# Filter stage of a spectral mixer: inverse step five groups behind, five buffers, earlier weight split, a new order of the last groups

## The chip, the cores and the metric

The kernel runs on one core of a Trainium2 chip. The metric is device time in microseconds of one execution. The core has five engines that run beside each other, each with its own queue worked off in order: TensorE (PE in the profile; PEld is its weight load), VectorE (DVE), ScalarE (ACT), GpSimd (POOL), and SyncE (SP), which here only issues DMAs. TensorE writes its products to PSUM, which the kernel uses as four tiles; ACT and DVE read them, POOL does not in this kernel.

## The reference

Four layers on x of 2048 x 640 float32: filter, MLP, filter, MLP, each with a layer norm ahead and a residual. Only the filter's part is touched.

```python
def _A_ref(x, w_r, w_i):
    W = w_r + 1j * w_i
    X = jnp.fft.rfft2(x, axes=(-2, -1)) * W
    return jnp.fft.irfft2(X, s=(S, D), axes=(-2, -1))
x = x + _A_ref(_layernorm(x), A_w_r, A_w_i)
x = x + _B_ref(_layernorm(x), B_w1, B_b1, B_w2, B_b2)   # twice, both
```

## The kernel before

Transforms are products with tables of cosines and sines, and each operand is split into a float16 high part and a float16 low part (h and l), so that three products give about float32. Sums in PSUM are float32.

The filter of one layer is made in three steps. `a0` (before, and inside the MLP stage ahead of the second filter) makes the first factor of the transform over the 2048 rows. `a1`, the stage that is changed, runs over NG = 16 groups of rows; for each group g it makes the transform over the 640 columns, the second factor over the rows, the product with the filter, and the inverse of the second row factor. `a2` then makes the inverse over the columns and the last inverse factor, adds the residual and normalises for the MLP. `a1` and `a2` run once for each of the two filter layers; the last stage before the second `a1` is the end of the first MLP.

In `a1` one group goes through these steps, named by functions inside it:

- `dstage(g)`: TensorE, columns, from `s1h`, `s1l` and the small stack `stk`; result in PSUM.
- `psplit`: ACT makes `ph`, DVE makes `pl` from that PSUM tile.
- `s2stage(g)`: TensorE, forward step over rows (table `tS2`).
- `terms`: DVE, two passes over PSUM with the filter `w` and a scale `sx`, into `ta`, `tb`; `sums`: POOL, two passes, real and imaginary part of the product.
- `xhi`: ACT, `xh`; `xlo`: POOL, `xl`; `twice`: ACT, a copy of 63 columns inside `xh` (0) or `xl` (1), which the inverse needs twice.
- `is2stage(g)`: TensorE, inverse step over rows (table `tI2`, 36 products with half of the rows each), into PSUM.
- `yhi`: ACT, `Yh`; `ylo`: DVE, two passes, `Yl`. All groups' Y together are the operand of `a2`, whose first product (`id_mm(0)`) therefore waits for the last group.

The loop is software-pipelined and its order is fixed: while `self.pin` is set, each engine's instructions keep the order of the program. DMAs of SP are not pinned; a planner places them. In the pass g of the loop (g = 0 to 14) TensorE does `dstage(g+1)`, `is2stage(g-3)`, `s2stage(g)`; ACT `xhi(g-2)`, its copy, `ph` of g+1, `yhi(g-3)`, the copy of `xl`; POOL `xlo(g-2)`, `sums(g-1)`; DVE `terms(g-1)`, `pl` of g+1, `ylo(g-3)`. The tiles `xh`, `xl` have three buffers (`xs`, index g % 3). After the loop, groups 12 to 15 are still to be inverted; that end is written out by hand.

Beside this, the loop prepares the first weight tile of the MLP that follows: `wload(0)` loads it as two halves `raw`; in the first layer `scan1` squares each half on ACT and `scale_b` and `scale1` make a power of two as its scale, each with one tiny product with `ones` into a PSUM tile of its own and then a chain of tiny DVE operations; `wsplit` splits the tile in four quarters, `wh` on ACT and one pass later `wl` on DVE. The MLP's loads of tile 1 go into the same two `raw` buffers. PSUM tiles all come from one pool of four (`big`); a tile that is asked for waits until one has been read.

Of the kernel before, what the change touches and what calls it, by code (L numbers as in the profile page):

```python
# [12 lines left out]
AF = mybir.ActivationFunctionType  # L13
# [4 lines left out]
S, D, NL, F = 2048, 640, 321, 1728  # L18
NJ, NG, NFT = 16, 16, 14
NQ = 8  # L20
SEQ = [t + 7 * i for t in (0, 6, 1, 2, 3, 4, 5) for i in range(2)]
EPS = 1e-5
GC = 0.044715
# [34 lines left out]
class Layers:  # L58
# [41 lines left out]
    def setup(self):  # L100
# [16 lines left out]
        self.qt = base.tile([128, NFT], F32, name="qt")  # L117
        self.s2, self.c2 = (base.tile([128, NQ], F32, name=f"{a}p") for a in "sc")
        self.second, self.nr = False, 3
# [300 lines left out]
    def a1(self, first):  # L420
        nc, A = self.nc, self.A
        V, G, T = self.V, self.G, self.T
# [6 lines left out]
        self.tDi = pY.tile([128, 2, 3, 2, 322], F16, name=f"tDi{self.n}")  # L429
        p = self.push("a1", side=self.sp)  # L430
        xs = []
        for i in range(3):
            xh = p.tile([128, 2, 384], F16, name=f"xh{i}_{self.n}")
            xl = p.tile([128, 2, 384], F16, name=f"xl{i}_{self.n}")
            xs.append((xh, xl))
# [6 lines left out]
        def yparts(g, ps, lt):  # L442

            o = tuple(y[:, g, :, lt.start * 32:lt.stop * 32] for y in yv)
            return pairs(ps, lt.start * 128, lt.stop * 128), *o

        def yhi(g, ps, lt=slice(0, 3)):
            a, h, _ = yparts(g, ps, lt)
            T.activation(h, a, AF.Copy, scale=YC)

        def ylo(g, ps, lt=slice(0, 3)):
            a, h, l = yparts(g, ps, lt)
            for q in range(2):
                V.scalar_tensor_tensor(l[:, q], a[:, q], YC, h[:, q], op0=ALU.mult, op1=ALU.subtract)
# [46 lines left out]

        def xhi(g, c, x):

            return T.activation(xs[g % 3][0][:, :, c], x, AF.Copy)

        def xlo(g, c, x, W=G):

            xh, xl = (q[:, :, c] for q in xs[g % 3])
            return W.tensor_tensor(xl, x, xh, op=ALU.subtract)

        def twice(g, i):

            q = xs[g % 3][i]
            T.activation(q[:, :, NL:], q[:, :, 257:320], AF.Copy)

        def s2stage(g, ph, pl):
# [9 lines left out]
        def is2mm(ps, g, lt):  # L526

            sp = 1 if g == 0 else 0
            out = slice(128 * lt, 128 * lt + 128)

            for ri in range(2):
                for k, (a, b) in enumerate(((0, 0), (0, 1), (1, 0))):
                    for q in range(2):
                        r = slice(64 * q, 64 * q + 64)
                        mm(
                            ps[:, q, out], xs[g % 3][a][r, ri, out], self.tI2[r, b, sp, ri],
                            start=ri == 0 and k == 0, stop=ri == 1 and k == 2,
                        )

        def is2stage(g):  # L540
            ps = self.big()
            for lt in range(3):
                is2mm(ps, g, lt)
            return ps

        def s2mm(ps, x, lt):

            c = slice(128 * lt, min(128 * lt + 128, NL))
            for ri in range(2):
                for q in range(2):  # L550
                    a = tuple(self.tS2[:, h, 0, 2 * ri + q] for h in range(2))
                    self.mm3(ps[:, ri, c], a, tuple(b[:, q, c] for b in x), q == 0, q == 1)
# [8 lines left out]
        def sums(tt, c, W=G):  # L561

            ta, tb = (q[:, :, c] for q in tt)
            W.tensor_tensor(ta[:, 0], ta[:, 0], tb[:, 1], op=ALU.subtract)
            return W.tensor_tensor(ta[:, 1], tb[:, 0], ta[:, 1], op=ALU.add)
# [8 lines left out]
        quarter = lambda q: ((q // 2,), slice(q % 2 * 4, q % 2 * 4 + 4))  # L574

        self.pin = True
        every = slice(0, NL)
        w = {g: wload(g) for g in range(3)}
        pp, ps2, pv, ta = {}, {}, {}, {}
        ps = dstage(0)  # L580
        pp[0] = tuple(self.t(p, [128, 2, 322], F16, a, 2) for a in ("ph", "pl"))
        sc = PQS / (S1S * TS)
        for q in range(2):
            a, b, c = ps[:, q, :NL], pp[0][0][:, q, :NL], pp[0][1][:, q, :NL]
            T.activation(b, a, AF.Copy, scale=sc)
            V.scalar_tensor_tensor(c, a, sc, b, op0=ALU.mult, op1=ALU.subtract)
        for g in range(NG - 1):
            q = psplit(dstage(g + 1))
            if g > 2:
                pv[g - 3] = is2stage(g - 3)  # L590
            ps2[g] = s2stage(g, *pp.pop(g))
            i = g % NC
            if i:
                stack(g + 3)
            k = g - 1
            if first and g == 0:
                for _ in self.scale_x(p):
                    pass
            if k > 0:
                xhi(k - 1, every, ta[k - 1])  # L600
                twice(k - 1, 0)
                xlo(k - 1, every, ta.pop(k - 1))
            if k >= 0:
                tt = terms(ps2.pop(k), k, w[k])
                ta[k], gi = tt[0], sums(tt, every)
            next(q)
            pp[g + 1] = next(q)
            if 10 <= g < 14:
                self.wsplit(0, quarter(g - 10)[0], hi=False, part=quarter(g - 10)[1])
            if k == 3:  # L610
                with self.after(gi):
                    nc.gpsimd.dma_start(self.tDi, A["tDi"])
                    nc.gpsimd.dma_start(self.tIM0, A["tIM"][:, 0:4])
            if g > 2:
                yhi(g - 3, pv[g - 3])
                ylo(g - 3, pv.pop(g - 3))
            if k > 0:
                twice(k - 1, 1)
            if k >= 0 and g + 2 < NG:
                w[g + 2] = wload(g + 2)  # L620
            if g == 3:
                self.wload(0)
                self.wopen(0)
            if first and g == 4:
                sb = self.scale_b()
            if first and 4 <= g < 8:
                next(sb)
            if first and g in (5, 6):
                self.scan1(0, (g - 5,))
            if first and g == 7:  # L630
                sc0 = self.scale1(0)
            if first and 7 <= g < 10:
                next(sc0)
            if 9 <= g < 13:
                self.wsplit(0, quarter(g - 9)[0], lo=False, part=quarter(g - 9)[1])

        k = NG - 2
        parts = slice(0, 256), slice(256, NL)
        h = self.big()
        for lt in range(3):  # L640
            s2mm(h, pp[k + 1], lt)
        xhi(k - 1, every, ta[k - 1])
        twice(k - 1, 0)
        xlo(k - 1, every, ta.pop(k - 1))
        tt = terms(ps2.pop(k), k, w[k])
        ta[k] = tt[0]
        sums(tt, every)
        twice(k - 1, 1)
        pv[k - 2] = is2stage(k - 2)
        tt = [self.t(p, [128, 2, NL], F32, a, n) for a, n in (("ta", 3), ("tb", 2))]  # L650
        for c in parts:
            for i, q in enumerate(tt):
                filtered(q[:, :, c], h[:, :, c], k + 1, w[k + 1][:, :, c], i)
            sums(tt, c, V if c.start else G)
        xhi(k, every, ta[k])
        twice(k, 0)
        yhi(k - 2, pv[k - 2])
        pv[k - 1] = is2stage(k - 1)
        for c in parts:
            xhi(k + 1, c, tt[0][:, :, c])  # L660
            xlo(k + 1, c, tt[0][:, :, c], V)
        twice(k + 1, 0)
        xlo(k, every, ta.pop(k))
        ylo(k - 2, pv.pop(k - 2))
        twice(k, 1)
        twice(k + 1, 1)
        pv[k] = is2stage(k)
        yhi(k - 1, pv[k - 1])
        ylo(k - 1, pv.pop(k - 1))
        h = [self.big() for _ in parts]  # L670
        is2mm(h[0], k + 1, 0)
        is2mm(h[0], k + 1, 1)
        yhi(k, pv[k])
        ylo(k, pv.pop(k))
        is2mm(h[1], k + 1, 2)
        for q, lt in zip(h, (slice(0, 2), slice(2, 3))):
            yhi(k + 1, q, lt)
            ylo(k + 1, q, lt)
# [130 lines left out]
    def wtile(self, m):  # L809

        k, i = m // NFT, m % NFT if m < NFT else m - NFT
        if self.second:
            i = i // 2 + i % 2 * NQ if k else SEQ[i]
        return min(k, 1), i, NFT if k else NJ
# [282 lines left out]
    def b2nd(self, li):  # L1097
# [17 lines left out]
        for j in range(NJ):  # L1115
            self.h.append((self.hh[j], ph.tile([128, 2, 320], F16, name=f"hl{j}_{self.n}")))
            V.tensor_tensor(self.h[j][1], self.hf[j], self.hh[j], op=SUB)
        V.tensor_tensor(self.s2, self.st[1][:, :NQ], self.st[1][:, NQ:], op=ALU.min)
        V.tensor_tensor(self.c2, self.ct[1][:, :NQ], self.ct[1][:, NQ:], op=ALU.max)
        self.pin = False  # L1120
# [19 lines left out]
        UB = {a: i for i, a in enumerate(("B11", "B21", "B22", "T1", "T2", "T3", "T4"))}  # L1140
        ops = [(d, *q) for d in range(NQ) for q in PQ]
        NP = len(ops)
# [67 lines left out]

        dup = lambda m: SEQ[m] == NFT - 1

# [19 lines left out]
        for m in range(NFT):  # L1232
            t, k = SEQ[m] % 7, SEQ[m] // 7
            if m < 2:
# [8 lines left out]
            for j in run:  # L1243
# [8 lines left out]
                if m == NFT - 1 and j in (1, 4, 7, 10):  # L1252
# [434 lines left out]
```

## Time and profile before

| what | us |
|---|---|
| three runs | 1034.32, 1034.83, 1036.58; median 1034.83 |
| profiled execution, its own time | 1035.71 |
| its span, first to last instruction | 1033.9 |
| first `a1`: first column product to the next stage's first product | 60.6 to 135.5 |
| second `a1` | 567.7 to 638.8 |
| busy in the span: PE, DVE, ACT, POOL | 987.5, 724.0, 571.2, 263.8 |
| granted TensorE clock, mean over the span | 0.977 |

How to read the rows that follow. A timeline row is start, duration, engine, line, operation, output<-inputs, shapes, count; in brackets the idle time of that engine just before and what ended it. Nearly all rows have line 50, the line of a helper through which pinned instructions are recorded, so they are told apart by the names of their tiles: `ta`, `tb` are the filter's terms, `ps` a PSUM tile. A row of the chain of waits is start, duration, what. A row of stretches has the stretch, its length, busy time and count for PE, PEld, DVE, ACT, POOL, then the granted clock, the DMA share and GB/s. Ends of matmuls are modelled, and neighbouring instructions overlap a little, so durations here are taken from start to start.

### The profile page before, as it was taken

Reading aid. Unit: us, or ns where it says so; the run is one execution under the profiler, and the core shown is the slowest. Engines: PE = TensorE matmul, PEld = TensorE weight load, DVE = VectorE, ACT = ScalarE, POOL = GpSimd, SP = SyncE. Lnnn points to the kernel's source line nnn. Section 1 sums busy time; section 2 is a strip of 40 time slices with the busy share of each in tenths; the row PEclk is TensorE's granted clock in tenths of the full one; section 3 lists DMA queues with packets and bytes.
Section 4 is the critical chain, followed back from the end, with each engine's and each line's share of the span. In section 5 each row is a group of like instructions: output and inputs, shape, how many; then the busy total and the mean of one; then the engine's idle time right before and its main releaser. Section 6 shows DMA issues by size and latency. Waiting matters only on the chain.

```text
span 1033.9 us, 20948 instructions
## 1 busy us (share of the span) xinstructions
PE 987.5 (96%) x8379; PEld 737.1 (71%) x8379; DVE 724.0 (70%) x1424; ACT 571.2 (55%) x874; POOL 263.8 (26%) x436
## 2 busy tenths in 40 slices
PE   4879989999999999999997998999999999999998
PEld 3767767677777777777775887776777777777776
DVE  7978968954333956666675797897654564988885
ACT  4847668675554556555542475784544454534541
POOL 6928747500000002222112575770000000000000
PEclk9599999999999999999998999999999999999999
DMA  7765356622222264444412644655322232445411
GB/s 227 276 180 165 109 160 220 209 85 93 78 79 75 71 237 146 138 135 123 123 59 73 195 148 132 199 186 196 127 85 82 73 107 78 140 153 174 163 44 52
DMA packets 55738, 139.48 MB, mean 135 GB/s; under 512 B 6461, under 2 KB 12249, under 8 KB 55641
## 3 DMA queue, kind: packets, MB, share of 16 engines
q1 hardware_dynamic: 54200, 131.97, 39.7%
q0 software_dynamic: 1440, 6.17, 1.9%
q8 instruction: 66, 1.08, 0.4%
q14 instruction: 32, 0.25, 0.1%
HBM read 115.05 MB, written 23.07 MB: 134 GB/s over the span
## 4 chain that ended last, share of the span: by engine, by line
PE 55%; DVE 18%; ACT 9%; POOL 8%; issue 5%; DMA 4%; SPq 0%; ACTq 0%; POOLq 0%; DVEq 0%
PE ps L50 55%; DMA xt<-x 4%; DVE wl L50 3%; DVE st L50 3%; DVE f L50 2%; DVE s1l L50 2%; POOL eo L50 2%; POOL ta L50 2%; DVE xt L50 2%; ACT wh L50 2%; POOL xt L50 1%; ACT z L50 1%; ACT junk L50 1%; DVE hl L50 1%; ACT eh L50 1%
## 5 line engine op out<-in xcount | busy, mean ns | idle before, releaser
L50 PEld LDWEIGHTS <-wh 128*128 128x128 f16 x2992 | 289.7, 98 | 113.1 <-issue 1.8
L50 PEld LDWEIGHTS <-wl 128*128 128x128 f16 x1616 | 157.9, 98 | 62.4 <-DVE wl L50 0.9
L50 PE MATMUL ps<-hh,wh 128*128 128x320 f16 x896 | 186.5, 299 | 0.7 <-ACT hh L50 0.6
L50 PE MATMUL ps<-hl,wh 128*128 128x320 f16 x896 | 184.7, 299 | 0.0
L50 PE MATMUL ps<-hh,wl 128*128 128x320 f16 x832 | 171.5, 299 | 0.5 <-DVE wl L50 0.5
L50 DVE SCALAR_TENSOR_TENSOR wl<-raw,s,wh 128x1024 f16<-128x1024 f32 (+2 forms) x88 | 105.3, 1201 | 87.6 <-ACT wh L50 87.5
L50 PE MATMUL ps<-uh,wl 128*128 128x320 f16 x448 | 133.1, 299 | 0.0
L50 PE MATMUL ps<-ul,wh 128*128 128x320 f16 x448 | 133.1, 299 | 0.0
L50 ACT ACTIVATE wh<-raw,s 128x1024 f16<-128x1024 f32 (+2 forms) x92 | 94.7, 1047 | 68.4 <-PE ps L50 61.6
L50 PE MATMUL ps<-uh,wh 128*128 128x320 f16 x416 | 124.3, 299 | 0.0
L50 ACT ACTIVATE junk<-raw 128x896 bf16<-128x896 f32 (+1 forms) x60 | 59.6, 994 | 45.5 <-DMA raw<-w 45.4
L50 PE MATMUL ps<-tDi,Yh 128*128 128x322 f16 x320 | 71.6, 301 | 0.4 <-ACT Yh L50 0.4
L50 POOL TENSOR_TENSOR r<-v,mh 128x1 f32<-128x1 f32 x64 | 37.3, 584 | 133.6 <-DVE nm L50 123.3
L50 PE MATMUL ps<-u,wo 128*128 128x320 f16 x504 | 69.9, 299 | 0.0
L50 DVE TENSOR_TENSOR f<-eo 128x256 f32<-128x256 f32 (+1 forms) x124 | 39.0, 368 | 41.9 <-POOL eo L50 41.2
L50 PEld LDWEIGHTS <-wo 128*128 128x128 f16 x504 | 49.3, 98 | 19.1
L50 POOL TENSOR_TENSOR xt<-xt,ec 128x320 f32<-128x320 f32 x64 | 52.4, 840 | 38.6 <-DVE xt L50 38.5
L50 DVE BATCH_NORM_STATS2 st<-xt 128x6 f32<-128x320 f32 x126 | 55.3, 481 | 6.3 <-DMA xt<-x 5.2
L50 ACT ACTIVATE z<-xt,nb,r 128x640 f32<-128x640 f32 x31 | 28.5, 919 | 56.0 <-POOL z L50 43.5
L50 PE MATMUL ps<-tM,f 128*128 128x128 f32 x160 | 38.3, 415 | 21.5 <-DMA xt<-x 12.2
L50 PE MATMUL ps<-ph,tS 128*128 128x321 f16 (+2 forms) x288 | 58.0, 286 | 0.1
L50 POOL TENSOR_TENSOR eo<-z 128x320 f32<-128x320 f32 x62 | 53.2, 880 | 17.1 <-ACT z L50 15.1
(175 smaller groups left out, 1880.6 us busy)
## 6 DMA issues: line engine op xcount, KB each, us to landing
raw<-w SPq DMA_DIRECT2D x56, 512.0 KB
xt<-x SPq DMA_DIRECT2D x79, 320.0 KB
w<-w SPq DMA_DIRECT2D x48, 321.0 KB
x<-xt SPq DMA_DIRECT2D x47, 320.0 KB
raw<-w SPq DMA_DIRECT2D x32, 448.0 KB
raw<-w2z SPq DMA_DIRECT2D x32, 448.0 KB
out<-xt SPq DMA_DIRECT2D x15, 320.0 KB
tIM<-tIM POOLq DMA_DIRECT2D x8, 512.0 KB, 5.6
```

What stands on the lines that cost most here:

```text
L50: i = f(*a, **k)
```

## The change

The inverse step, `Yh` and `Yl` follow five groups behind instead of three (`LAG`), `xs` has five buffers (`NX`). The load of weight tile 0, its squares, its scale and its split move two passes ahead; `scale_b`, and the DMAs that POOL issues in the loop, stay. After the loop six groups, 10 to 15, are to be inverted, and the order of that end is new: two inverse steps stand before the sums of group 14, each `Yh`, `Yl` pair (`back`) stands between the steps of groups 14 and 15, the upper columns of group 15 go ahead of the lower ones.

```diff
+LAG, NX = 5, 5
-        for i in range(3):
+        for i in range(NX):
             xh = p.tile([128, 2, 384], F16, name=f"xh{i}_{self.n}")
...
-            return T.activation(xs[g % 3][0][:, :, c], x, AF.Copy)
+            return T.activation(xs[g % NX][0][:, :, c], x, AF.Copy)
...
-            if g > 2:
-                pv[g - 3] = is2stage(g - 3)
+            if g >= LAG:
+                pv[g - LAG] = is2stage(g - LAG)
...
-            if 10 <= g < 14:
-                self.wsplit(0, quarter(g - 10)[0], hi=False, part=quarter(g - 10)[1])
+            if 8 <= g < 12:
+                self.wsplit(0, quarter(g - 8)[0], hi=False, part=quarter(g - 8)[1])
...
-            if g > 2:
-                yhi(g - 3, pv[g - 3])
-                ylo(g - 3, pv.pop(g - 3))
+            if g >= LAG:
+                yhi(g - LAG, pv[g - LAG])
+                ylo(g - LAG, pv.pop(g - LAG))
...
-            if g == 3:
+            if g == 1:
                 self.wload(0)
                 self.wopen(0)
...
-            if first and g in (5, 6):
-                self.scan1(0, (g - 5,))
-            if first and g == 7:
+            if first and g in (3, 4):
+                self.scan1(0, (g - 3,))
+            if first and g == 5:
                 sc0 = self.scale1(0)
-            if first and 7 <= g < 10:
+            if first and 5 <= g < 8:
                 next(sc0)
-            if 9 <= g < 13:
-                self.wsplit(0, quarter(g - 9)[0], lo=False, part=quarter(g - 9)[1])
+            if 7 <= g < 11:
+                self.wsplit(0, quarter(g - 7)[0], lo=False, part=quarter(g - 7)[1])
...
+        def back(n):
+            yhi(n, pv[n])
+            ylo(n, pv.pop(n))
+
+        n = k - LAG + 1
...
+        pv[n] = is2stage(n)
+        pv[n + 1] = is2stage(n + 1)
         sums(tt, every)
         twice(k - 1, 1)
-        pv[k - 2] = is2stage(k - 2)
         tt = [self.t(p, [128, 2, NL], F32, a, n) for a, n in (("ta", 3), ("tb", 2))]
         for c in parts:
             for i, q in enumerate(tt):
                 filtered(q[:, :, c], h[:, :, c], k + 1, w[k + 1][:, :, c], i)
-            sums(tt, c, V if c.start else G)
+        sums(tt, parts[1], V)
+        back(n)
+        pv[n + 2] = is2stage(n + 2)
+        sums(tt, parts[0])
         xhi(k, every, ta[k])
         twice(k, 0)
-        yhi(k - 2, pv[k - 2])
-        pv[k - 1] = is2stage(k - 1)
-        for c in parts:
-            xhi(k + 1, c, tt[0][:, :, c])
+        xhi(k + 1, parts[1], tt[0][:, :, parts[1]])
+        twice(k + 1, 0)
+        back(n + 1)
+        pv[n + 3] = is2stage(n + 3)
+        xlo(k, every, ta.pop(k))
+        xhi(k + 1, parts[0], tt[0][:, :, parts[0]])
+        back(n + 2)
+        for c in parts[::-1]:
             xlo(k + 1, c, tt[0][:, :, c], V)
-        twice(k + 1, 0)
-        xlo(k, every, ta.pop(k))
-        ylo(k - 2, pv.pop(k - 2))
         twice(k, 1)
         twice(k + 1, 1)
+        back(n + 3)
         pv[k] = is2stage(k)
-        yhi(k - 1, pv[k - 1])
-        ylo(k - 1, pv.pop(k - 1))
         h = [self.big() for _ in parts]
         is2mm(h[0], k + 1, 0)
         is2mm(h[0], k + 1, 1)
-        yhi(k, pv[k])
-        ylo(k, pv.pop(k))
         is2mm(h[1], k + 1, 2)
+        back(k)
         for q, lt in zip(h, (slice(0, 2), slice(2, 3))):
             yhi(k + 1, q, lt)
             ylo(k + 1, q, lt)
```

More of the change, by code (lines that the diff above doesn't have):

```diff
@@ L502, in xhi @@
         def xhi(g, c, x):
-            return T.activation(xs[g % 3][0][:, :, c], x, AF.Copy)
+            return T.activation(xs[g % NX][0][:, :, c], x, AF.Copy)
         def xlo(g, c, x, W=G):
-            xh, xl = (q[:, :, c] for q in xs[g % 3])
+            xh, xl = (q[:, :, c] for q in xs[g % NX])
             return W.tensor_tensor(xl, x, xh, op=ALU.subtract)
         def twice(g, i):
-            q = xs[g % 3][i]
+            q = xs[g % NX][i]
             T.activation(q[:, :, NL:], q[:, :, 257:320], AF.Copy)
@@ L535, in is2mm @@
                         mm(
-                            ps[:, q, out], xs[g % 3][a][r, ri, out], self.tI2[r, b, sp, ri],
+                            ps[:, q, out], xs[g % NX][a][r, ri, out], self.tI2[r, b, sp, ri],
                             start=ri == 0 and k == 0, stop=ri == 1 and k == 2,
```

## The prediction

> **What bounds the kernel now.** I read the page first, then the chain of waits through both filter stages, then the engines' timelines there. On the page TensorE is busy 96% of the span, and both filter stages end in a hole of it. A pass is one turn of the loop over g; X is the moment at which a pass starts its `xl` on POOL.
>
> ```profile
> PE 987.5 (96%) x8379; PEld 737.1 (71%) x8379; DVE 724.0 (70%) x1424; ACT 571.2 (55%) x874; POOL 263.8 (26%) x436
> ```
>
> The chain of waits, second filter stage (start, us, what): in the loop it runs from POOL's sums to ACT's `xh`, to POOL's `xl` and to sums again, and not through TensorE; it comes back to TensorE at 640.04, with the next stage's first products.
>
> ```profile
> 627.84 1.47 POOL ta L50 x2
> 629.33 0.75 ACT xh L50
> ...
> 640.04 5.03 PE ps L50 x35
> ```
>
> Undisturbed this ring takes 3.69 us a pass, as POOL's timeline shows, each `xl` waiting for ACT:
>
> ```profile
> 89.64 1.42 POOL L50 TENSOR_TENSOR xl<-ta,xh 128x642 f16<-128x642 f32 x1 [0.85 <-ACT xh L50]
> ...
> 93.33 1.42 POOL L50 TENSOR_TENSOR xl<-ta,xh 128x642 f16<-128x642 f32 x1 [0.85 <-ACT xh L50]
> ...
> 601.74 1.42 POOL L50 TENSOR_TENSOR xl<-ta,xh 128x642 f16<-128x642 f32 x1 [0.85 <-ACT xh L50]
> ```
>
> TensorE's own pass is longer: forward step over s from 599.01, column step (D) from 600.66, inverse step (I) from 601.90, forward step again from 603.01. That is 4.00 us, 1.11 of it inverse step.
>
> ```profile
> 599.01 0.31 PE L50 MATMUL ps<-ph,tS 128*128 128x321 f16 x1
> ...
> 600.66 0.30 PE L50 MATMUL ps<-tD,s1h 128*128 128x160 f16 x2
> ...
> 601.90 0.29 PE L50 MATMUL ps<-tI,xh 64*128 64x128 f16 x4
> ...
> 603.01 0.31 PE L50 MATMUL ps<-ph,tS 128*128 128x321 f16 x1
> ```
>
> So TensorE falls 0.31 us a pass behind the ring and at last holds it: ACT waits 0.41 for an inverse step, with a weight split and the next `xh` queued behind it. Later VectorE paces the passes with a weight quarter, 4.15 us from `pl` to `pl` (619.17 to 623.32), with no idle time in between.
>
> ```profile
> 607.13 0.81 ACT L50 ACTIVATE Yh<-ps 128x768 f16<-128x768 f32 x1 [0.41 <-PE ps L50]
> ```
> ```profile
> 619.17 0.82 DVE L50 SCALAR_TENSOR_TENSOR pl<-ps,ph 128x642 f16<-128x642 f32 x1
> 619.90 0.97 DVE L50 SCALAR_TENSOR_TENSOR wl<-raw,s,wh 128x512 f16<-128x512 f32 x1
> 620.80 1.01 DVE L50 SCALAR_TENSOR_TENSOR Yl<-ps,Yh 128x384 f16<-128x384 f32 x2
> 621.73 0.87 DVE L50 SCALAR_TENSOR_TENSOR ta<-ps,sx,w 128x642 f32<-128x642 f32 x1
> ...
> 623.32 0.81 DVE L50 SCALAR_TENSOR_TENSOR pl<-ps,ph 128x642 f16<-128x642 f32 x1
> ...
> 629.11 0.87 DVE L50 SCALAR_TENSOR_TENSOR ta<-ps,sx,w 128x642 f32<-128x642 f32 x1
> ...
> 632.99 0.67 DVE L50 TENSOR_TENSOR ta<-tb,ta 128x65 f32<-128x65 f32 x1
> 635.35 0.94 DVE L50 TENSOR_TENSOR xl<-ta,xh 128x512 f16<-128x512 f32 x2 [1.69 <-ACT xh L50]
> 636.22 4.16 DVE L50 SCALAR_TENSOR_TENSOR Yl<-ps,Yh 128x384 f16<-128x384 f32 x10
> ```
>
> **The loop, second stage.** Passes 3 and 4 lose their inverse step, so TensorE gains 2 x 1.11 = 2.2 us of lead. It loses 0.31 a pass from pass 5 on, so the lead lasts seven passes, to pass 12, and the slower weight passes stretch that. Hence ACT no longer waits at 607.13. Up to pass 8 (X = 601.74) nothing changes, since the ring sets those passes. The four weight passes are now 8 to 11: 4 x 4.15 brings X to 618.3, two ring turns of 3.69 to 625.7 in pass 14. `pl` follows X by 0.89 (94.22, in the fence of the first stage below, after 93.33), and `ta` of group 14 follows `pl` by 0.73 + 0.93 (619.17 to 619.90, 620.80 to 621.73): 628.2 against 629.11, 0.9 gained. Bounds: nothing (if the quarters alone made the old passes late) and 1.4 (if the first of the four costs the ring its 3.69 alone).
>
> **The last groups, second stage.** Count from that `ta` (t = 0; PE resumed at 640.04, so 10.93 before). VectorE now has five groups of `Yl` at 0.93 (620.80 to 621.73) instead of three. Until 4.55 its order is the old one (632.99 + 0.67). `Yl` 10 fills the old hole, 4.55 to 5.48. From here ACT sets the time:
>
> ```profile
> 633.02 0.74 ACT L50 ACTIVATE xh<-ta 128x642 f16<-128x642 f32 x1 [1.10 <-POOL ta L50]
> 633.80 0.31 ACT L50 ACTIVATE xh<-xh 128x126 f16<-128x126 f16 x1
> 634.01 0.79 ACT L50 ACTIVATE Yh<-ps 128x768 f16<-128x768 f32 x1
> 634.70 0.83 ACT L50 ACTIVATE xh<-ta 128x512 f16<-128x512 f32 x2
> ```
>
> By starts: a whole `xh` 0.78, a copy 0.21, a `Yh` 0.69 (its output after 0.79), the two parts of `xh` 15 0.83, with the wait of a copy for its input 0.86, which I part into 0.34 and 0.52. ACT starts `xh` 14 at 3.91 as before; then copy, small part, copy bring it to 5.45; `Yh` 11 is out at 6.24, so VectorE idles 0.76; large part, `Yh` 12 out at 7.45, VectorE idles 0.28 after `Yl` 11; `Yl` 12 ends at 8.38; `xl` 15 takes 0.87 (635.35 to 636.22), to 9.25. The copy of `xl` 15 stands ahead of `Yh` 13 in ACT's queue and waits for the small part, so `Yh` 13 is out only at 9.7: idle 0.45. Then `Yl` 13, `Yl` 14, and 0.76 for the first part of `Yl` 15: 12.35, TensorE at 12.4. So this end is 1.47 longer: 1.86 more `Yl`, and an idle of 1.69 and some crumbs exchanged for 1.49. Bounds: -0.1 (no idle at all: 4.55 + 5 x 0.93 + 0.87 + 0.76 = 10.83) and +2.0 (none of the old idle recovered). Queued behind the late `Yh` 13 are `Yh` 14 and 15; for them wait `Yl` and then TensorE.
>
> **First stage.** Its end went from 125.22 to 136.31, 11.09, so 12.4 is 1.31 longer. Its loop has one thing more: the scale of weight tile 0.
>
> ```profile
> 90.83 0.17 PE L50 MATMUL ps<-sqb,ones 128*128 128x1 bf16 x1
> 91.42 0.30 PE L50 MATMUL ps<-tD,s1h 128*128 128x160 f16 x2 [0.42 <-DVE pl L50]
> ...
> 91.28 1.01 DVE L50 SCALAR_TENSOR_TENSOR Yl<-ps,Yh 128x384 f16<-128x384 f32 x2
> ...
> 93.00 0.88 DVE L50 SCALAR_TENSOR_TENSOR tb<-ps,sx,w 128x642 f32<-128x642 f32 x1
> 94.22 0.83 DVE L50 SCALAR_TENSOR_TENSOR pl<-ps,ph 128x642 f16<-128x642 f32 x1 [0.34 <-ACT ph L50]
> ...
> 95.89 0.15 DVE L50 TENSOR_SCALAR qb<-ps 128x1 f32<-128x1 f32 x1
> ...
> 98.89 1.02 DVE L50 SCALAR_TENSOR_TENSOR Yl<-ps,Yh 128x384 f16<-128x384 f32 x2 [0.17 <-ACT Yh L50]
> ...
> 102.93 1.02 DVE L50 SCALAR_TENSOR_TENSOR Yl<-ps,Yh 128x384 f16<-128x384 f32 x2 [0.39 <-ACT Yh L50]
> ...
> 125.22 0.87 DVE L50 SCALAR_TENSOR_TENSOR ta<-ps,sx,w 128x642 f32<-128x642 f32 x1
> ...
> 136.31 7.40 PE ps L50 x52
> ```
>
> One small product (`ones`) took a PSUM tile at 90.83 and VectorE read it only at 95.89, five microseconds later; already for one such tile the next D waited 0.42 for a tile to come free. The move puts a second one, for weight 0, beside it in pass 6, and VectorE reads both at the end of pass 7: till then two of four tiles are gone. The second takes the tile that let D go at 91.42. D, I and S of pass 7 are queued behind it on TensorE and get tiles one by one: D when `Yl` is through (91.28 + 0.93, 92.2), I when `tb` is (93.00 + 0.88, 93.9). I ends at 95.0 and `Yh` at 95.9, where `Yl` could have begun at 94.96, right behind `pl`: 0.9 late, and with it `Yl`, the scale of weight 0, the first `wh` and the ring. The waits of `Yl` for TensorE, 0.17 and 0.39, go: 0.6 gained. So this loop is 0.3 longer; bounds -0.6 (tiles free themselves sooner), and +1.3 if the clock halves as well:
>
> ```profile
> 52.73:56.14 3.41, 1.87 (x12) 1.49 (x13) 3.34 (x11) 2.51 (x6) 2.08 (x5) 1.00 0.64 160
> 56.14:59.56 3.42, 3.42 (x18) 3.42 (x17) 3.35 (x9) 1.42 (x3) 0.00 (x0) 0.50 0.72 227
> ...
> 633.00:636.41 3.41, 1.09 (x34) 0.93 (x36) 1.72 (x5) 3.06 (x8) 3.21 (x9) 1.00 0.02 8
> 636.41:639.82 3.41, 3.02 (x48) 2.16 (x42) 3.27 (x8) 2.61 (x5) 0.00 (x0) 0.50 0.56 156
> ```
>
> The stretches are 3.41 us, PE busy comes first, the granted clock third from the end. Stretches with 1.87 and 1.09 us busy are each followed by one at half clock. The held tiles leave the stretch 90.28 to 93.69 with D alone, 1.3 us: I expect half clock after it, so that I takes 2.2 us instead of 1.11 and 1.0 more reaches the ring. [...]
>
> **At nothing.** Five buffers: no `xh` waits for a buffer now. POOL's order is untouched. The earlier load of tile 0: SP issued it at 38.11 already, far ahead of the loop that asks for it, so the place of the call doesn't set its time; the loads of tile 1, queued on the freed halves, go some 8 us sooner, long before their use. Moved squares and splits lie on ACT, which waits 1.10 for POOL where nothing else stands before `xh` (633.02); without that cover a square, 1024 wide, would cost the ring about 1.2 us, estimated from the 0.74 of the 642 wide `xh`.
>
> ```profile
> 38.11 0.43 SPq L822 DMA_DIRECT2D raw<-w  x1
> ```
>
> **Sum.** Second stage -0.9 + 1.47; first +0.3 + 1.31 + 1.0: +3.2 us. It is made against the profiled execution, 1035.71 us with a span of 1033.9, so 1038.9 there; that execution is 0.9 above the median of 1034.83, and put on the median it is 1038.0.
>
> **Rivals.** (1) The tiles cost nothing: a free one is found and the clock stays. Then -0.6 + 1.31 - 0.9 + 1.47 = +1.3, 1036.1, no measurable change. For it: the one tile held till 95.89 cost TensorE only 0.42. (2) Faster: ACT keeps ahead of VectorE in the last groups, which then cost 10.83 in each stage (-0.1, -0.2), and the loops gain 0.9 and 0.6; with the first quarter free, 0.5 more each: -1.8 to -2.8, about 1032.4. It decides at `Yh` 11: out before 5.5. Against it: four ACT instructions stand ahead of it. (3) Half clock at the start of the next stage: the last 5 us of the new end hold only the inverse step of group 15, about 1.6 us busy, under 1.87; the next 3.41 us are then at half clock, and some 2.5 of them fall on the next stage's first products: 1.25 us lost in each stage, 1040.5. Before, the slowed steps 14 and 15 kept 636.41 to 639.82 busy, so the clock was back in time. (4) The later inverse step doesn't free TensorE, because it waits for `pl` in the loop anyway: +2.8 for the ends and 1.0 for the tiles' delay, with no gain of the loops: 1038.6, inside the forecast's own range.
>
> **Numbers.** Forecast with (4) 0.45 (own range 1036.6 to 1039.3), (1) 0.24, (2) 0.15, (3) 0.16. Under 0.2% (2.1 us) a measurement can't tell a change; faster is (2), 0.16; same is (1), 0.24; slower the rest, 0.60. The range reaches from the lower half of (1) to just past (3): 1033.4 to 1041.0.
>
> **What would show it.** Right: in both stages TensorE's time from `ta` 14 to the next stage grows by over 1 us, with ACT named ahead of `Yl` 11 and 13; no ACT wait on TensorE in passes 8 to 10; two `ones` products side by side and a hole after them. Wrong: `Yl` 10 to 15 without idle, or a first loop that ends sooner.

## The result, and the profile after

| | runs | median, us | range, us |
|---|---|---|---|
| before | 4 | 1035.27 | 1034.32 to 1036.58 |
| after | 4 | 1044.24 | 1043.15 to 1045.99 |

The ratio is 1.0078, with a 95% interval of 1.0059 to 1.0098: the change made the kernel 9 us slower, where 3.2 were forecast. The profiled execution of after took 1045.99 us with a span of 1044.2, the longest of the four, so 10.24 us of span are to be found in it (1044.17 against 1033.94). Nearly all engines' busy time stayed what it was:

```profile
PE 994.8 (95%) x8379; PEld 739.7 (71%) x8379; DVE 723.2 (69%) x1424; ACT 569.5 (55%) x874; POOL 264.7 (25%) x436
```

TensorE alone is busy longer, by 7.3 us for the same 8379 products. That is the first sign of slower products rather than of more waiting.

**Where the time lies.** Eight marks divide the span. They are, in each of the two stages, the first column step D on TensorE, `ta` 14 on VectorE, the next stage's first product with Yl on TensorE, and the fifth `eh` on ScalarE, behind which the two kernels run step for step. The timelines of before give the marks that the prediction's fences lack, then come those of after (start, us, engine, helper's line, operation):

```profile
60.62 0.32 PE L50 MATMUL ps<-tD,s1h 128*128 128x160 f16 x2 [0.80 <-ACT s1h L50]
...
150.12 0.78 ACT L50 ACTIVATE eh<-ps,cxe 128x644 fp32r<-128x644 f32 x1
...
567.69 0.45 PE L50 MATMUL ps<-tD,s1h 128*128 128x160 f16 x2 [0.37 <-ACT s1h L50]
...
653.91 0.78 ACT L50 ACTIVATE eh<-ps,cxe 128x644 fp32r<-128x644 f32 x1
```
```profile
60.41 0.32 PE L51 MATMUL ps<-tD,s1h 128*128 128x160 f16 x2 [0.80 <-ACT s1h L51]
...
126.65 0.88 DVE L51 SCALAR_TENSOR_TENSOR ta<-ps,sx,w 128x642 f32<-128x642 f32 x1
...
139.18 0.45 PE L51 MATMUL ps<-tDi,Yl 128*128 128x322 f16 x1 [0.74 <-DVE Yl L51]
...
155.49 0.78 ACT L51 ACTIVATE eh<-ps,cxe 128x644 fp32r<-128x644 f32 x1
...
574.49 0.45 PE L51 MATMUL ps<-tD,s1h 128*128 128x160 f16 x2 [0.37 <-ACT s1h L51]
...
634.87 0.87 DVE L51 SCALAR_TENSOR_TENSOR ta<-ps,sx,w 128x642 f32<-128x642 f32 x1
...
647.41 0.45 PE L51 MATMUL ps<-tDi,Yl 128*128 128x322 f16 x1 [0.86 <-DVE Yl L51]
...
663.89 0.78 ACT L51 ACTIVATE eh<-ps,cxe 128x644 fp32r<-128x644 f32 x1
```

The differences of these starts:

| part | before | after | difference | forecast |
|---|---|---|---|---|
| first stage, loop (D to `ta` 14) | 64.60 | 66.24 | +1.64 | +1.3 |
| first stage, end (`ta` 14 to first Yl product) | 11.09 | 12.53 | +1.44 | +1.31 |
| start of the next stage (to the fifth `eh`) | 13.81 | 16.31 | +2.50 | 0 |
| from there to the second stage's D | 417.57 | 419.00 | +1.43 | 0 |
| second stage, loop | 61.42 | 60.38 | -1.04 | -0.9 |
| second stage, end | 10.93 | 12.54 | +1.61 | +1.47 |
| start of the next stage | 13.87 | 16.48 | +2.61 | 0 |

What lies ahead of the first row and behind the last adds -0.21 and +0.25. The four forecast rows sum to +3.65 against +3.18. The rest is in three rows for which the forecast had nothing.

**The loop of the first stage**, TensorE's timeline of after, pass 7, and VectorE's where the weight's scale is read:

```profile
90.15 0.17 PE L51 MATMUL ps<-sqb,ones 128*128 128x1 bf16 x1
91.45 0.16 PE L51 MATMUL ps<-sqb,ones 128*128 128x1 bf16 x1 [1.14 <-DVE pl L51]
92.38 0.31 PE L51 MATMUL ps<-tD,s1h 128*128 128x160 f16 x2 [0.77 <-DVE Yl L51]
...
94.00 0.39 PE L51 MATMUL ps<-tI,xh 64*128 64x128 f16 x4
...
96.98 1.02 DVE L51 SCALAR_TENSOR_TENSOR Yl<-ps,Yh 128x384 f16<-128x384 f32 x2 [1.31 <-ACT Yh L51]
```

The windows of after, one for each stretch of the clock (length, busy PE and how many products, then the other engines; the granted clock is third from the end):

```profile
89.73:93.15 3.42, 1.52 (x18) 1.16 (x16) 2.81 (x6) 2.32 (x5) 2.77 (x3) 1.00 1.01 329
93.15:96.56 3.41, 3.41 (x47) 2.72 (x45) 1.59 (x2) 1.56 (x4) 2.82 (x3) 0.50 0.41 111
```

Two `ones` products side by side, then D held until a `Yl` frees a PSUM tile, a stretch with 1.52 us of work, and the inverse step in the next stretch, at half clock. D was forecast for 92.2, the inverse step for 93.9, `Yl` for 95.9 and, with the half clock, 96.9; they came at 92.38, 94.00 and 96.98.

**The loop of the second stage.** In before ScalarE waited 0.41 for an inverse step ahead of `Yh` (607.13, shown with the prediction); in its timeline of after none of the ten `Yh` of that loop (597.80 to 633.06) waits; two of them:

```profile
609.13 0.80 ACT L51 ACTIVATE Yh<-ps 128x768 f16<-128x768 f32 x1
613.26 0.80 ACT L51 ACTIVATE Yh<-ps 128x768 f16<-128x768 f32 x1
```

**The end of the second stage**, VectorE's timeline of after, from `Yl` 10 on:

```profile
639.42 1.01 DVE L51 SCALAR_TENSOR_TENSOR Yl<-ps,Yh 128x384 f16<-128x384 f32 x2
641.22 1.02 DVE L51 SCALAR_TENSOR_TENSOR Yl<-ps,Yh 128x384 f16<-128x384 f32 x2 [0.79 <-ACT Yh L51]
642.44 1.02 DVE L51 SCALAR_TENSOR_TENSOR Yl<-ps,Yh 128x384 f16<-128x384 f32 x2 [0.20 <-ACT Yh L51]
643.38 0.88 DVE L51 TENSOR_TENSOR xl<-ta,xh 128x130 f16<-128x130 f32 x2
644.74 3.01 DVE L51 SCALAR_TENSOR_TENSOR Yl<-ps,Yh 128x384 f16<-128x384 f32 x8 [0.47 <-ACT Yh L51]
```

The waits ahead of `Yl` 11, 12 and 13 are 0.79, 0.20 and 0.47, all for ScalarE's `Yh`; 0.76, 0.28 and 0.45 were forecast.

**The start of the next stage**, again in windows of the clock's stretches, after:

```profile
639.29:642.70 3.41, 1.99 (x60) 1.50 (x56) 2.42 (x6) 3.25 (x8) 2.25 (x8) 1.00 0.02 5
642.70:646.11 3.41, 1.70 (x46) 1.30 (x46) 2.94 (x7) 2.41 (x5) 0.17 (x1) 1.00 0.00 0
646.11:649.53 3.42, 2.56 (x11) 1.19 (x9) 1.64 (x6) 0.06 (x1) 0.40 (x1) 0.50 0.56 152
649.53:652.94 3.41, 3.41 (x14) 1.96 (x13) 0.73 (x1) 0.80 (x1) 0.00 (x0) 0.50 0.02 6
652.94:656.35 3.41, 3.41 (x27) 2.58 (x24) 1.22 (x3) 1.24 (x2) 0.00 (x0) 1.00 0.00 0
```

Here are the missing 2.6 us. A lean stretch (1.70) is followed not by one stretch at half clock but by two: the first of them contains the wait for the last `Yl`, and the clock comes back only behind the second, which is busy throughout. Fourteen products fit into 649.53 to 652.94, where the next has 27, and TensorE is what limits this stage (3.41 us busy of 3.41 in both). The first stage shows the same, with 1.58 us busy ahead of two stretches at half clock.

**Between the stages.** The +1.43 appears in the first MLP. ScalarE's timeline shows its first `xt` there waiting for a load, in before and then in after:

```profile
386.99 1.65 ACT L50 ACTIVATE xt<-xt,b2s 128x640 f32<-128x640 f32 x2 [6.44 <-DMA xt<-x]
```
```profile
393.38 1.63 ACT L51 ACTIVATE xt<-xt,b2s 128x640 f32<-128x640 f32 x2 [7.46 <-DMA xt<-x]
```

What follows kept the lag. From the MLP's first `hl` to the `xt` that VectorE makes behind this load took 191.59 in before and 192.61 in after, 1.02 more, and between 190.20 and 192.95 in the twelve executions profiled below; 190.20 is the changed kernel itself. The other 0.41 comes between that `xt` and the second stage (179.84 before, 180.25 after, 179.79 to 180.01 in the twelve). The first is inside the spread. The second, 180.25, is just outside it, but the changed kernel run again has 179.90, and 416.28 for the whole row where its first run has 419.00. So the +1.43 belongs to this execution and not to the change; what sets the load's time is open.

### The profile page after: what moved, and what is told of

Read it like the earlier page. It is cut to its first block, busy times and chain, and to the rows that moved or that the text cites. A ratio compares the mean times of both kernels' runs of the same rounds, so it can differ in the third digit from the quotient of the medians.

```text
span 1044.2 us, 20935 instructions
## 1 busy us (share of the span) xinstructions
PE 994.8 (95%) x8379; PEld 739.7 (71%) x8379; DVE 723.2 (69%) x1424; ACT 569.5 (55%) x874; POOL 264.7 (25%) x436
## 3 DMA queue, kind: packets, MB, share of 16 engines
HBM read 115.05 MB, written 23.07 MB: 132 GB/s over the span
## 4 chain that ended last, share of the span: by engine, by line
PE 49%; DVE 18%; POOL 11%; ACT 10%; DMA 6%; issue 5%; SPq 0%; ACTq 0%; POOLq 0%; DVEq 0%
PE ps L51 49%; DMA xt<-x 4%; POOL ta L51 3%; DVE wl L51 3%; DVE st L51 3%; POOL eo L51 2%; POOL xl L51 2%; DVE xt L51 2%; ACT xh L51 2%; DVE f L51 2%; POOL xt L51 2%; DVE s1l L51 2%; ACT wh L51 2%; ACT z L51 1%; DVE Yl L51 1%
## 5 line engine op out<-in xcount | busy, mean ns | idle before, releaser
L51 PE MATMUL ps<-tDi,Yh 128*128 128x322 f16 x320 | 75.9, 315 | 1.1 <-ACT Yh L51 1.1
L51 PE MATMUL ps<-tDi,Yl 128*128 128x322 f16 x192 | 58.4, 312 | 1.6 <-DVE Yl L51 1.6
```

What stands on the lines that cost most here:

```text
L51: i = f(*a, **k)
```

## The experiments

Each group of runs had runs of the kernel before beside it on the same chip, and ratios are to those. These groups ran on three chips, and of the kernel before there is one profile, that of the first table. Times of the profile are the marks of the table above; "to the fifth `eh`" is end and start together, counted from `ta` 14 (24.90 and 24.80 in before, 28.85 and 29.02 in after).

**Small products that fill TensorE's waits (fill_after).**

```diff
+    def idle(self, ps, n):
+        for _ in range(n):
+            self.PE.matmul(ps[:, 1, 384:512], self.ones, self.ones, start=True, stop=True)
...
+        self.idle(h[0], 26)
         is2mm(h[0], k + 1, 0)
         is2mm(h[0], k + 1, 1)
         is2mm(h[1], k + 1, 2)
+        self.idle(h[1], 10)
...
+                    if j == lt == ty == 0:
+                        mm(ps[:, 0, :322], a[0], b[0], start=True, stop=False)
+                        mm(ps[:, 0, :322], a[0], b[1], start=False, stop=False)
+                        self.idle(ps, 24)
+                        mm(ps[:, 0, :322], a[1], b[0], start=False, stop=False)
+                    elif lt < 2:
```

> The changed kernel with small products of ones by ones (128x128, not used by anything) put on TensorE at the end of both filter stages: 26 ahead of the inverse step of group 15, 10 behind it, 24 inside the first product of the next stage, between its two Yh products and its first Yl product. They keep TensorE busy where it waited. Theory A (the two stretches at half clock at the start of the next stage cost about 2.5 us each): no half clock there, 1044.2 - 5 = 1039 to 1040. Rival B (Yl and the loads set the start of the next stage, and the half clock only shows there): 1043.5 to 1045.

Measured: 1039.15 us, ratio 1.0026 (1.0014 to 1.0037), against 1.0078. The time to the fifth `eh` is 26.76 and 26.75, though the ends themselves grew by 0.4 (12.96 and 12.95 to the first Yl product): the starts are 13.80 both, as in before (13.81 and 13.87). The windows around the second stage's end:

```profile
634.20:637.61 3.41, 2.02 (x61) 1.53 (x57) 2.43 (x6) 3.17 (x8) 2.18 (x8) 1.00 0.00 0
637.61:641.02 3.41, 3.41 (x80) 3.10 (x77) 2.93 (x8) 2.31 (x4) 0.00 (x0) 1.00 0.02 5
641.02:644.44 3.42, 3.42 (x43) 2.83 (x41) 1.55 (x6) 0.39 (x1) 0.57 (x1) 1.00 0.55 147
```

No lean stretch, no half clock. Products that nothing uses, put where TensorE waited, took 2.5 and 2.7 us off the starts. That is theory A's picture, and rival B's 1043.5 or more is missed. How much the whole kernel gained is less sure: 5 us by the ratio of the first runs, 2 us by that of the changed kernel run again (1.0045, below).

**The same on the kernel before (fill_before).** The edit is the same at the same three places.

> The kernel before with the same small products at the same three places: the control. Its half clock lies at 131.24 to 134.65 and 636.41 to 639.82, over before the next stage starts, and comes from a lean stretch ahead of where the products are put. Theory A: it stays, and the time is 1035.3 within 0.7. Rival B: the same. If small products cost or gain something by themselves, it shows here.

Measured: 1042.01 us, ratio 1.006 (1.0042 to 1.0077): both theories missed. TensorE's timeline shows why:

```profile
134.24 2.96 PE L50 MATMUL ps<-ones 128*128 128x128 bf16 x26
138.80 0.73 PE L50 MATMUL ps<-ones 128*128 128x128 bf16 x10
```

In before the parts of group 15 are ready when TensorE gets there, so the small products stand ahead of real work, and 26 of them took 2.96 us at half clock (0.111 each by starts, 134.24 to 137.13, against 0.057 for the ten behind the step, 138.80 to 139.37). The end grew from 11.09 to 15.05 and from 10.93 to 13.69. As a control it is spoilt; what it shows is that here, where TensorE did not wait, filling cost time. The profile, of the slowest of the six executions, holds one thing more: its first loop took 66.87 against 64.60, though the edit lies behind it. Two stretches at half clock, from 59.84 and from 70.08, fell into the first passes. So the first loop, counted from D, varies by over 2 us without any change to it.

**The weight tile's steps alone (mlp_only).** On the kernel before, the load of tile 0 in pass 1, squares in 3 and 4, scale from 5 to 7, quarters from 7 on.

```diff
-            if 10 <= g < 14:
-                self.wsplit(0, quarter(g - 10)[0], hi=False, part=quarter(g - 10)[1])
+            if 8 <= g < 12:
+                self.wsplit(0, quarter(g - 8)[0], hi=False, part=quarter(g - 8)[1])
...
-            if first and g == 7:
+            if first and g == 5:
                 sc0 = self.scale1(0)
```

> The kernel before with one part of the change alone: load, squares, scale and split of weight tile 0 two passes sooner; inverse step three groups behind, old order of the end. Theory A (two ones products held two PSUM tiles and the half clock follows, +1.9 in the first stage's loop, nothing in the second): 1037.2. Rival B (the tiles cost nothing, the loss of the first loop came from the five groups): 1035.3 within 0.5.

Measured: 1036.93 us, ratio 1.0004 (0.9993 to 1.0014). The medians show no loss, and the interval allows at most 1.5 us. In the profile the first loop is 66.30, against 64.60 in before and 66.24 in after, which looks like theory A's loss but mostly isn't. VectorE's `ta` of group 0, before and then mlp_only, splits the loop:

```profile
70.38 0.88 DVE L50 SCALAR_TENSOR_TENSOR ta<-ps,sx,w 128x642 f32<-128x642 f32 x1
```
```profile
71.15 0.88 DVE L50 SCALAR_TENSOR_TENSOR ta<-ps,sx,w 128x642 f32<-128x642 f32 x1
```

From D (60.62 and 60.12) to this `ta` mlp_only lost 1.27 of the 1.70, in a stretch at half clock. The moved steps are not the reason: best3 below, which has them too, takes 9.76 there, as before does. From there to `ta` 14 it took 55.27, against 54.84 in before and 56.27 in after. TensorE's D of pass 7 and the windows of mlp_only:

```profile
93.14 0.31 PE L50 MATMUL ps<-tD,s1h 128*128 128x160 f16 x2 [0.77 <-DVE Yl L50]
```
```profile
60.29:63.70 3.41, 3.00 (x23) 2.73 (x22) 0.63 (x1) 2.15 (x6) 0.00 (x0) 0.50 0.87 313
...
91.01:94.42 3.41, 2.21 (x24) 1.61 (x22) 3.10 (x5) 2.23 (x5) 2.56 (x4) 1.00 0.88 281
94.42:97.84 3.42, 2.94 (x49) 2.17 (x48) 2.13 (x6) 1.72 (x3) 2.51 (x3) 1.00 0.40 102
```

D is held for a `Yl` as in after, but the stretch around it holds 2.21 us of work, not 1.52, and no half clock follows. best3 has the same loop with the two `ones` products apart and took 54.34 from `ta` 0 on: the held tiles by themselves cost 0.93, and without them the moved steps gain 0.5 over before. In the second stage of mlp_only a stretch with 1.61 us of work is followed by half clock, and the start is 15.54: the old end can bring it on too.

**Those steps undone in the changed kernel (mlp_old).**

> The changed kernel with that part undone: load, squares, scale and split of weight tile 0 at the passes of before; five groups and the new order stay. Theory A: the first loop has no hole at pass 7 and no half clock after it, 1.4 to 2 us less in the first stage, 1042.3 to 1042.8, with both stretches of half clock at the start of the next stage still there. Rival B: 1044.2.

Measured: 1040.43 us, ratio 1.0044 (1.0029 to 1.006). The first loop is 64.67, 1.57 less than in after, as theory A says; from `ta` 0 on it is 54.87, no better than before (54.84), so the five groups by themselves gain nothing in the first loop. The ratio is under 1.0078, but no lower than that of the changed kernel run again (1.0045), so the medians don't settle what the undoing is worth. The ends are 12.44 and 12.46 and the starts 15.55 and 15.32: both half clocks are there, each somewhat cheaper.

**ScalarE's order in the end (end_early).**

```diff
         sums(tt, parts[0])
+        yhi(n + 1, pv[n + 1])
         xhi(k, every, ta[k])
...
-        back(n + 1)
+        ylo(n + 1, pv.pop(n + 1))
         pv[n + 3] = is2stage(n + 3)
+        yhi(n + 2, pv[n + 2])
         xlo(k, every, ta.pop(k))
         xhi(k + 1, parts[0], tt[0][:, :, parts[0]])
-        back(n + 2)
+        ylo(n + 2, pv.pop(n + 2))
+        yhi(n + 3, pv[n + 3])
...
         twice(k + 1, 1)
-        back(n + 3)
+        ylo(n + 3, pv.pop(n + 3))
```

> The changed kernel with ScalarE's order in the last groups altered: Yh 11 ahead of xh 14, Yh 12 ahead of the large part of xh 15, Yh 13 ahead of the two copies of xl 15. Theory (the longer end is ScalarE's order: VectorE waits 0.79, 0.20 and 0.47 for Yh there, in both stages): the time from ta 14 to the next stage's first Yl product falls from 12.53 to about 11.3, 1.2 less a stage: 1041.8, and lower if the two stretches at half clock get shorter with it. Rival (the five groups of Yl are the length of the end, the waits would only move): 12.3 or more, 1044.

Measured: 1036.72 us, ratio 0.9999 (0.9988 to 1.001): as fast as before. VectorE's timeline, second stage, has no wait left, six calls of `Yl` for groups 10 to 12 in a row:

```profile
633.36 3.00 DVE L51 SCALAR_TENSOR_TENSOR Yl<-ps,Yh 128x384 f16<-128x384 f32 x6
636.28 0.88 DVE L51 TENSOR_TENSOR xl<-ta,xh 128x130 f16<-128x130 f32 x2
637.09 3.06 DVE L51 SCALAR_TENSOR_TENSOR Yl<-ps,Yh 128x384 f16<-128x384 f32 x8
```

The ends are 11.00 and 10.99. The theory stands, and the gain is larger than it: to the fifth `eh` it is 24.81 and 24.80, four us less than after in each stage, of which 1.5 is the order and 2.5 the half clock, which did not come. That it stayed away fits the fuller end, in which no stretch holds under 2.27 us of work.

**The two `ones` products apart (scale_apart).**

```diff
-            if first and g == 4:
+            if first and g == 2:
                 sb = self.scale_b()
-            if first and 4 <= g < 8:
+            if first and 2 <= g < 6:
                 next(sb)
```

> The changed kernel with the square and the ones product of the bias two passes sooner still, so that the two ones products stand in passes 4 and 6 instead of both in pass 6. Theory (the two held PSUM tiles make the hole in pass 7, and the half clock follows it): from the first column step to ta 14 of the first stage 64.7 to 65.2 instead of 66.24, so 1 to 1.5 less, 1042.7 to 1043.2. Rival (the weight quarters in passes 7 to 10 cost the time, not the tiles): 66.2, 1044.2.

Measured: 1039.54 us, ratio 1.0022 (1.0009 to 1.0035). The first loop is 63.99, 2.25 less than in after and more than expected; from `ta` 0 on it is 54.16 against 56.27. The whole gained more than the loop: the first stage's start is 13.82, without a half clock, and the second's 16.45, with two, though the end is unaltered. With one product in pass 6, D follows it at once in TensorE's timeline:

```profile
90.19 0.17 PE L51 MATMUL ps<-sqb,ones 128*128 128x1 bf16 x1
90.29 0.30 PE L51 MATMUL ps<-tD,s1h 128*128 128x160 f16 x2
```

The rival, that the quarters cost the time, falls: they are where they were in after.

**Products with Yh first (hifirst_after, hifirst_before).** The first product of the next stage is real work that can fill the wait for `Yl`:

```diff
+            if j == 0:
+                for d in range(2):
+                    for lt in range(3):
+                        for ty in range(2):
+                            y = self.Y[d][:, lt, ty, j]
+                            for h in (d,) if lt == 2 else range(2 - d):
+                                mm(
+                                    ps[:, ty, :322], y, self.tDi[:, h, lt, ty],
+                                    start=d == lt == h == 0, stop=d == 1 and lt == 2,
+                                )
+                return ps
```

> The changed kernel with the first product of the next stage in another order: all ten products with Yh first, then the six with Yl, so that TensorE has work while the last Yl is made. Theory A (half clock): the lean stretch ahead of it stays, so one stretch of half clock stays, but the second goes: 2.2 less a stage, 1039.8. Rival B (the start of the next stage hangs on Yl): 0.7 a stage at most, 1042.8 or more.

> The kernel before with the same other order of that first product: TensorE waits 0.36 and 0.34 us there, and the products with Yh fill the wait: 0.7 less a stage, a ratio of 0.9987. If the order costs something by itself, it is slower here.

Measured: hifirst_after 1038.64 us, ratio 1.0017 (1.0007 to 1.0026), a little faster than theory A has it; 25.25 and 27.45 to the fifth `eh`. But the profile doesn't show theory A's one stretch of half clock a stage: there is none at the first stage's end, and two at the second's, 638.54 to 645.37, of which the first lies over the end. hifirst_before 1033.71 us, ratio 0.9964 (0.9951 to 0.9977), better than expected; 24.22 and 23.71 against 24.90 and 24.80, so 1.8 us of it are seen in the profile; where the rest of the 3.6 lies is open. TensorE's timeline of hifirst_before shows the product without a wait:

```profile
134.70 1.77 PE L50 MATMUL ps<-tDi,Yh 128*128 128x322 f16 x10
136.31 0.99 PE L50 MATMUL ps<-tDi,Yl 128*128 128x322 f16 x6
```

**The changed kernel again (after_again).**

> The changed kernel once more, unaltered, on the same chip as the next three, since the times of both kernels spread by several microseconds from run to run. If the spread comes from where the 3.41 us stretches of the clock fall against the kernel, the four spans from the start of the first column step to the end shift by what the stretches at half clock cost (0 to 2.6 us each) and nothing else. Ratio expected 1.006 to 1.009.

Measured: 1041.26 us, 1039.78 to 1045.09, ratio 1.0045 (1.0029 to 1.0062): less than the first time, and below what was expected. The profiled execution, one of the shorter ones (1040.26), has the loops at 66.28 and 60.72 and the ends at 12.53 and 12.54, as in the first; but the starts are 13.83 and 15.32 instead of 16.31 and 16.48. The part between the stages is 2.72 shorter, so the expectation that nothing else would shift was wrong. The windows of its first stage:

```profile
133.38:136.79 3.41, 1.87 (x58) 1.44 (x52) 2.74 (x7) 2.31 (x6) 0.59 (x6) 1.00 0.02 2
136.79:140.21 3.42, 1.85 (x16) 1.07 (x13) 2.44 (x7) 0.86 (x3) 0.22 (x1) 1.00 0.96 313
140.21:143.62 3.41, 3.41 (x26) 2.60 (x25) 0.89 (x1) 1.20 (x2) 0.00 (x0) 1.00 0.84 299
```

The same end, with the same waits, is cut at other places; no stretch holds less than 1.85 us of work, and no half clock follows. In its second stage a stretch at 1.64 is followed by two at half clock, the first of which lies mostly over the end; the start is 1.5 longer there:

```profile
635.14:638.55 3.41, 1.64 (x40) 1.15 (x40) 2.43 (x7) 2.31 (x6) 1.25 (x6) 1.00 0.02 5
638.55:641.97 3.42, 2.61 (x34) 1.75 (x34) 2.94 (x7) 2.68 (x5) 0.37 (x1) 0.50 0.00 0
641.97:645.38 3.41, 3.13 (x12) 1.79 (x13) 0.61 (x3) 0.00 (x0) 0.20 (x1) 0.50 0.50 154
```

So the extra of 0 to 2.6 us a stage goes by where the stretches fall, and that differs from execution to execution. mlp_old and scale_apart have the same end; over the two runs of the changed kernel and these two, six of the eight starts are 1.45 to 2.61 longer than in before, and two are not.

**Filling ahead of the start alone (fill_15).** The 26 and the 10 products without the 24.

> The changed kernel with the small products ahead of and behind the inverse step of group 15 alone (26 and 10), none inside the next stage's first product. Theory A (a stretch at half clock follows a lean one): the stretch ahead of the next stage is no longer lean, so at most one half stretch stays, behind the wait for Yl, and it costs less: from ta 14 to the fifth eh 26.5 to 27.5 instead of 28.9, 1039.5 to 1041.5. Rival B (it hangs on Yl): 28.9, 1044.

Measured: 1038.46 us, ratio 1.0017 (1.0008 to 1.0026); to the fifth `eh` 26.35 and 26.34, under the lower end of theory A. In this execution no half clock came behind either end, and both ends are 12.54, as long as in after: these products cost nothing. Rival B had 28.9. The changed kernel run again was on the same chip, and the intervals do not overlap: 1.0045 (1.0029 to 1.0062) against 1.0017. Products that nothing uses saved 2.8 us, so the half clock is a cause and not a symptom.

**Versions from the parts (best5, best3).**

> The changed kernel with three things together: the two ones products in passes 4 and 6, ScalarE's order in the last groups with Yh 11, 12 and 13 sooner, and the first product of the next stage with its Yh products first. From the parts: first loop 64.0, ends to the fifth eh 24.0 each, second loop 60.6; about 5.5 us under the kernel before on the same chip, a ratio of 0.9945.

> The kernel before (three groups, three buffers, old order of the end) with weight tile 0 two passes sooner, the two ones products in passes 4 and 6, and the Yh products first. It tells what the five groups and the new order are worth beside best5: if they free TensorE in the loop, best5 is faster by 0.7 to 1.5 us; if not, the two agree. Expected ratio 0.9955.

Measured: best5 1033.56 us, ratio 0.9964 (0.995 to 0.9977); best3 1032.85 us, ratio 0.996 (0.9946 to 0.9975). Both beat both kernels, best5 by less than expected. They agree, so following five groups behind is worth nothing over the whole that these runs can tell. By the profiles best5 is 1.5 shorter in the second loop (60.45 against 61.95) and 0.9 longer in the second stage to the fifth `eh` (23.93 against 23.07); in the first stage 0.1 and 0.5 shorter. hifirst_before, with one edit, is as good within the intervals.

## Why the prediction was right or wrong

The direction was right, and the time, 1044.24, lay outside the range of 1033.4 to 1041.0. The signs named for a right forecast all came: the ends over 1 us longer with ScalarE named, no wait of it in the second loop, two `ones` products with a hole behind them. What failed is a term that was left at nothing: the half clock at the start of the next stage.

- **The loop of the second stage** (-0.9): -1.04, with ScalarE's waits gone, as the prediction had it. The second loops of all kernels bear it out: 61.3 to 62.1 in the five with three groups, 60.3 to 60.9 in the nine executions with five groups.
- **The ends** (+1.47, +1.31): +1.61 and +1.44. The reckoning through ScalarE's queue met each of the three waits within 0.08, and end_early shows that ScalarE's order is the cause of the longer end: without the waits five groups of `Yl` take 11.0, what three took before. The lower bound of 10.83 was nearly reached.
- **The loop of the first stage** (+0.3 and +1.0): +1.64, of which 0.21 lie ahead of `ta` 0. The held tiles and the half clock behind them came where they were put, and in about the sizes that were reckoned: 0.93 for the tiles (mlp_only against best3, forecast 0.9), 1.00 more with the half clock (after against mlp_only, forecast 1.0; 0.9 to 1.3 over the six profiles with it). The gain of 0.6 was given the wrong source. It was ascribed to the later inverse step, but five groups alone gain nothing there (mlp_old), while the moved steps with the tiles free gain 0.5 with three groups (best3) and 0.7 with five (scale_apart).
- **Rival (1)**, tiles that cost nothing: wrong, since D was held till 92.38 and half clock followed; scale_apart took both away. **Rival (2)**: at its stated point `Yh` 11 was late, and it fell; end_early is that rival made true by hand. **Rival (4)**: wrong, since the second loop gained.
- **Rival (3) is what happened**, and it is the step that failed. The prediction had its mechanism and its condition ("the last 5 us of the new end hold only the inverse step of group 15, about 1.6 us busy"; 1.58 and 1.70 were measured), yet gave it 0.16 and left it out of the sum, and priced it at 1.25 a stage, from one stretch of which 2.5 us fall on the next stage. There were two stretches, since the first contains the wait for `Yl`, and the price was 2.50 and 2.61. That is 5.1 of the 6.6 us between 3.65 and 10.24; another 1.4 is the variation between the stages.
- The prediction treated this half clock as there or not there. after_again shows that it is a matter of each execution: 0 and 1.5 in one, 2.50 and 2.61 in the other. The mean of these four is 1.65; added in both stages it makes 6.5 of the forecast's 3.2, which lies between the two measurements of 9 and 4. That the 4 comes near 3.2 is luck: in its profile 1.5 of half clock stands against 1.3 less than before between the stages.
- In the prediction's chances faster stands at 0.16 where its rival (2) has 0.15, and slower at 0.60 where its parts make 0.61; nothing hangs on that.

## What to carry to other kernels

Where a stage ends in a chain over other engines, count TensorE's work per stretch of its clock (3.41 us here), over the end and over the start of the next stage: in after the lean ends, with 1.58 and 1.70 us of work in their last stretches, were followed by starts 2.50 and 2.61 us longer, which the ends' own lengths don't show. Before pulling work apart or adding lag, fill such an end with work of the next stage that is ready (here the products with Yh: ratio 0.9964 in hifirst_before), or order the engine that releases it by who waits (end_early: four us less than after in each stage); and don't let small results hold whole PSUM tiles side by side (0.93 us here, and 1.00 more with the half clock behind it). Judge such changes on several executions, since the stretches fall differently in each (the first start took 16.31 and 13.83 us in the two of the changed kernel).

## What the runs showed of the hardware

Each figure is TensorE's busy time in a stretch of 3.41 us. Around the ends of before, after, after_again and scale_apart, and in pass 7 of after, the stretches at full clock that stood ahead of half clock held 1.09 us (before, 633.00 to 636.41) to 1.70 us (after, 642.70 to 646.11); none was idle. After stretches with 1.84 (scale_apart, 133.73 to 137.14), 1.85 and 1.87 us (after_again, 133.38 to 140.21) the clock stayed full, and so it did after one with 1.69 (hifirst_after, 133.37 to 136.78). Ahead of the first column step and in the first passes, 1.87 was followed by half clock in before (52.73 to 56.14), 1.97 in after (52.19 to 55.60), 2.02 in mlp_only (53.46 to 56.87) and 1.98 in fill_before (66.67 to 70.08). At the end of the first MLP it followed 1.19 us of work in before (557.90 to 561.32) and an idle stretch in best5 (558.88 to 562.29, 0.00 us). So no one amount of work in a stretch divides the cases, and what sets the fall is not shown.

At half clock, around the ends of after, after_again and scale_apart, stretches with 2.47 to 2.62 us busy were followed by another half, those with 3.13 and more by full clock, as 2.95 and 3.02 were in before. Ahead of the first column step of before, 3.03 was followed by another half (32.25 to 35.66).

The two executions of the changed kernel have the same first end, 12.53 us, and starts of 16.31 and 13.83 us behind it: in the one the clock was 0.50 from 137.51 to 144.34, in the other it was 1.00 throughout (133.38 to 143.62).
